# Output sums of a Fourier filter and expert layer with the output weights stationary, turned back by transposing DMAs

## The chip, the cores and the metric

The kernel runs on one core of a Trainium2 chip. The metric is device time in microseconds of one execution, the median of the runs; the profile shows one further execution in detail. A core has a tensor engine (TensorE, "PE" in the profile, with its weight loads as "PEld"), VectorE ("DVE"), ScalarE ("ACT"), GpSimd ("POOL") and SyncE ("SP", which here only issues DMAs). Each takes its instructions from a queue of its own.

## The reference

```python
def _attn_ref(x, filt_r, filt_i):            # x: 8 x 3008 x 256
    X = np.fft.rfft(x, axis=1)
    Y = X * (filt_r + 1j * filt_i)[None, :, :]
    return np.fft.irfft(Y, n=x.shape[1], axis=1)

def _moe_ref(x, w_in, w_out, beta):          # x: 24064 x 256, w_in: 256 x 2048, w_out: 2048 x 256
    h = x @ w_in
    g = h * (1.0 / (1.0 + np.exp(-beta * h)))
    return g @ w_out
```

Each of 8 batches goes through a real Fourier transform along its 3008 tokens, a product with a filter, and the inverse transform. The 24064 tokens then go through a two-layer network with 2048 hidden features and the activation h times sigmoid(beta h).

## The kernel before

The network is the main loop. Tokens are taken in 47 blocks of 512 (`TB`), hidden features in 16 groups of 128 (`NFB`); one block and one group make a step, 752 steps in all. A step `s` computes `hps` (L785: two matmuls, `win_sb` stationary, 512 tokens moving), ScalarE turns it into `gT` (L794, features on partitions, tokens along the row), and two steps later, by `lags`, four matmuls (L803) add the group's share to the output: there the 128 x 128 piece of `gT` is stationary and `wout_sb` (256 columns) moves, so that tokens come out on the partitions of `acc`. After the last group of a block, `out_block` (L753) copies the two banks of `acc` to `ost` on VectorE (L757, shown as L112, the line of the helper) and stores them from SP (L762, L764). `acc` tiles come from a pool of three banks, two of which a block uses. The last block goes through `out_last` instead.

The Fourier work of the next batch is woven into the steps. A table `plan`, filled by `at(step, function, ...)`, is written out by hand (L687 to L735): `s1` (L565) is the first small transform, `a2_load` turns its result by eight transposing DMAs from SP (L581), `s2` (L592) is the second transform and the product with the filter on VectorE (L606, L607, L610), whose two halves are added on GpSimd into `yh` (L611), `s3` (L624) takes `yh` back and stores `z` to DRAM (L631), `zz_load` reads it back turned (L636), and `s4` (L646) makes the tokens of `y` that the main loop reads. Within a step the order of issue is `hps`, then what the plan has, then the output matmuls and, at the end of a block, `out_block`. The engines' queues follow that order. With o the first step of batch b - 1's tokens (0, 80, 176, 272, ... for b = 1, 2, 3, 4), batch b has its `s2` at o + 4, 8 and 12 in each of four blocks, its last `z` store at o + 66, `zz_load` at o + 70, `s4` from o + 80, and `a2_load` for b + 1 at o + 82. Batches 1 and 2 have steps of their own: `a2_load` at 16 and 80, `s2` from 23 and from 88, `zz_load` of batch 1 at 54. Loads of `x` (`load_x`, L171) are issued from GpSimd's queue.

The first batch is done before the steps begin. In that opening the filters, `win_sb` (L476) and the output weights are loaded; `load_wout` (L360) brings four groups of `moe_w_out` into a staging tile `ws` (two of them), `scale_wout` (L367) divides them by beta on GpSimd into `wout_sb`. `spin` (L271) issues filler matmuls on a tile of zeros.

Of the kernel before, what the change touches and what calls it, by code (L numbers as in the profile page):

```python
# [10 lines left out]
P = 128  # L11
# [4 lines left out]
F32 = mybir.dt.float32  # L16
BF16 = mybir.dt.bfloat16
I32 = mybir.dt.int32

TWO_PI = 2.0 * math.pi  # L20

# [15 lines left out]
def kernel(  # L37
# [10 lines left out]
    nc = tc.nc  # L48

    B, S, D = x.shape  # L50
# [20 lines left out]
    tw = dict(reuse_waits="tile")  # L71
# [29 lines left out]
    wout_sb = wpool.tile([P, NFB, D], BF16, name="wout_sb", tag="wout_sb")  # L101
# [4 lines left out]
    st = {}  # L106
# [162 lines left out]
    def spin(n, idle):  # L269
        for _ in range(n):  # L270
            nc.tensor.matmul(idle[:], lhsT=rest[:, :P], rhs=rest[:], start=True, stop=True)  # L271
# [73 lines left out]

    r_sq.close()

    wst = ctx.enter_context(tc.tile_pool(name="wstage", bufs=2, **tw))
    zzpool = ctx.enter_context(tc.tile_pool(name="zzpool", bufs=4, **tw))
    WG = 4  # L350
    wstage = {}

    def load_x(b, g):
        t = xpool.tile([KP, JG, D], BF16, name="xg", tag="xg")
        load_rows(t[:], b, g * JG, (g + 1) * JG)
        xg[b, g] = t

    def load_wout(f0):
        ws = wst.tile([P, WG, D], F32, name="ws", tag="ws")
        nc.sync.dma_start(  # L360
            ws[:],
            moe_w_out[f0 * P : (f0 + WG) * P, :].rearrange("(fb fp) j -> fp fb j", fp=P),
        )
        wstage[f0] = ws
# [117 lines left out]
    load_win(0, 4 * P)  # L482
    spread(4)
    spread(5)
    load_x(1, 0)
    load_win(4 * P, FF)
    for g in range(1, 4):
        load_x(1, g)
    load_wout(0)
    load_wout(WG)  # L490
    scale_wout(0)
    scale_wout(WG)

# [26 lines left out]
    def tail_tile(i, shape, dt=F32):  # L520
        return pair[i].tile(shape, dt, name="pt", tag=f"pt{i}")
# [10 lines left out]
    for e in range(NDC):  # L532
        for h in range(2):
# [1 line left out]
            f4(0, h, e, ps)  # L535
            f4_head(0, h, e, ps, e == 1 and h == 0)
            late.append((0, h, e, ps))
    spin(2, tail_tile(0, [P, 512]))
    z_evac(NUN - 1, 1, s5[1], JG, J, False)
    for a in late:  # L540
        f4_tail(*a, False)
# [145 lines left out]
    for b in range(1, B):  # L687
        o = first_step[b - 1]
        if b == 1:
            at(0, z_late, 1, 0)  # L690
            at(1, z_late, 1, 1)
            s1_steps(1, range(16), [3 + (2 * i + 1) // 3 for i in range(16)], False, (1, 4, 7, 10, 13))
            for i, r in enumerate((2, 3, 4, 5)):
                at(r, f_late, 1, i // 2, i % 2)
            for g in range(NG):
                at(o + 16, a2_load, 1, g)
            for hh, z0, f0 in ((2, (6, 9), (12, 15, 16, 17)), (3, (17, 18), (19, 20, 21, 22))):
                for e in range(NDC):
                    at(z0[e], z_late, hh, e)
                for i, r in enumerate(f0):  # L700
                    at(r, f_late, hh, i // 2, i % 2)
            s23_steps(1, [o + r for r in (23, 25, 27, 29, 31, 34, 36, 38, 40, 42, 44, 46)], 5, 1)
            for h in range(J // JG):
                at(o + 54, zz_load, 1, h)
            s4_steps(1, [o + 66 + (i * 12) // 15 for i in range(16)], 2)
            for f in (2, 3):
                at(f, load_wout, f * WG)
                at(f, scale_wout, f * WG)
            if B > 2:
                for g in range(4):  # L710
                    at(o + 24 + 3 * g, load_x, 2, g)
                late = (54, 55, 56, 57, 58, 59, 60, 61, 66, 67, 68, 70, 72, 73, 74, 76)
                s1_steps(2, range(16), [o + r for r in late], False)
                for g in range(NG):
                    at(o + 80, a2_load, 2, g)
                if B > 3:
                    for g in range(4):
                        at(o + (62, 68, 88, 92)[g], load_x, 3, g)
            continue
        base = [o + 16 * n + s for n in range(4) for s in (4, 8, 12)]  # L720
        if b == 2:
            base[:6] = [o + r for r in (8, 12, 19, 22, 26, 29)]
        s23_steps(b, base, 6, False)
        for h in range(J // JG):
            at(o + 70, zz_load, b, h)
        s4_steps(b, [o + 80 + (i * 13) // 15 for i in range(16)], False)
        if b + 1 < B:
            early = [o + 16 * n + s for n in range(4) for s in (7, 13)]
            late = [o + s for s in (66, 67, 69, 70, 72, 73, 75, 76)]
            s1_steps(b + 1, range(16), early + late, False)  # L730
            for g in range(NG):
                at(o + 82, a2_load, b + 1, g)
            if b + 2 < B:
                for g in range(4):
                    at(o + (30, 62, 88, 92)[g], load_x, b + 2, g)  # L735

    blk = {}
    acc = {}
    lags = {i: (2, 2, 2, 2) for i in range(NBLK)}
    lags[NBLK - 1] = (2, 2, 4, 6)  # L740
    outs = {}
    for s in range(NSTEP):
# [1 line left out]
        for tb, lag in enumerate(lags[i]):  # L744
            outs.setdefault(min(s + lag, NSTEP + max(1, tb)), []).append((i, fb, tb))

    def acc_of(i, tb):
        h = tb if i == NBLK - 1 and tb == 3 else tb // 2
        if (i, h) not in acc:
            acc[i, h] = opsum.tile([P, 2, D], F32, name="acc", tag="acc")  # L750
        return acc[i, h]

    def out_block(i):  # L753
        ost = ostp.tile([P, 4, D], F32, name="ost", tag="ost")
        rows = out[i * TB : (i + 1) * TB, :].rearrange("(c p) d -> p c d", p=P)
        for h in range(2):
            evac(ost[:, 2 * h : 2 * h + 2, :], acc[i, h][:], False)  # L757
        if i < HB:
            for h in range(2):
                off = (i * JG + 4 * h) * D  # L760
                dst = AP(out.tensor, out.offset + off, [[J * D, M], [D, 4], [1, D]])
                nc.sync.dma_start(dst, ost[h * M : (h + 1) * M, :, :])  # L762
            return
        nc.sync.dma_start(rows, ost[:])  # L764

    def out_last(i, tb, ost):
        rows = out[i * TB : (i + 1) * TB, :].rearrange("(c p) d -> p c d", p=P)
        if tb == 1:
            evac(ost[:, :2, :], acc[i, 0][:], True)
            nc.sync.dma_start(rows[:, :2, :], ost[:, :2, :])  # L770
        elif tb > 1:
            evac(ost[:, tb, :], acc_of(i, tb)[:, tb % 2, :], False)
            (nc.scalar if tb == 2 else nc.sync).dma_start(rows[:, tb, :], ost[:, tb, :])

    for s in range(NSTEP + 4):
        if s < NSTEP:
            i, fb = divmod(s, NFB)
            t0 = i * TB
            hps = hpsum.tile([P, TB], F32, name="hps", tag="hps")
            pos = t0  # L780
            while pos < t0 + TB:
                b, n0 = divmod(pos, S)
                ln = min(S - n0, t0 + TB - pos)
                for dc in range(NDC):
                    nc.tensor.matmul(  # L785
                        hps[:, pos - t0 : pos - t0 + ln],
                        lhsT=win_sb[:, dc, fb * P : (fb + 1) * P],
                        rhs=ys[b][:, dc, n0 : n0 + ln],
                        start=(dc == 0),
                        stop=(dc == NDC - 1),  # L790
                    )
                pos += ln
            gT = gpool.tile([P, TB], BF16, name="gT", tag="gT")
            nc.scalar.activation(gT[:], hps[:], ACT.Silu, scale=beta_sb[:, fb : fb + 1])  # L794
            blk[s] = gT
        for fn, a in plan.get(s, ()):
            fn(*a)
        last = NBLK - 1
        if s == NSTEP - 1:
            ost = ostp.tile([P, 4, D], F32, name="ost", tag="ost")  # L800
        for i, fb, tb in outs.get(s, ()):
            lone = i == last and tb > 1
            nc.tensor.matmul(  # L803
                acc_of(i, tb)[:, tb % 2, :],
                lhsT=blk[i * NFB + fb][:, tb * P : (tb + 1) * P],
                rhs=wout_sb[:, fb, :],
                start=(fb == 0 and (tb % 2 == 0 or lone)),
                stop=(fb == NFB - 1),
                skip_group_check=True,
            )  # L810
            if fb == NFB - 1:
                if i == last:
                    out_last(i, tb, ost)
                elif tb == 3:
                    out_block(i)
# [1 line left out]
_INS = ['x', 'filt_r', 'filt_i', 'moe_w_in', 'moe_w_out', 'moe_beta']  # L817
_OUTS = [((24064, 256), 'float32')]
# [25 lines left out]
```

## Time and profile before

| what | value |
|---|---|
| median of 3 runs (range) | 776.09 us (775.89 to 776.11) |
| the profiled execution | 776.16 us |
| its span, first to last instruction | 774.4 us |
| granted TensorE clock over the span | 1.000 |
| TensorE, VectorE, ScalarE, GpSimd busy | 99%, 56%, 71%, 20% |
| bytes moved by DMA | 77.74 MB |

A row of the profile's groups reads: line, engine, operation, what is written and read, shape, count, then busy time in us, mean ns of one, and the idle time of the engine just before, with what ended it. A row of a timeline reads: start in us, us from the first to the end of the last, engine, line, operation, tiles, count; the brackets give idle time before and what ended it. "SPq" is SP's queue issuing a DMA.

### The profile page before, as it was taken

Reading aid. Unit: us, or ns where it says so; the run is one execution under the profiler, and the core shown is the slowest. Engines: PE = TensorE matmul, PEld = TensorE weight load, DVE = VectorE, ACT = ScalarE, POOL = GpSimd, SP = SyncE. Lnnn points to the kernel's source line nnn. Section 1 sums busy time; section 2 is a strip of 40 time slices with the busy share of each in tenths; the row PEclk is TensorE's granted clock in tenths of the full one; section 3 lists DMA queues with packets and bytes.
Section 4 is the critical chain, followed back from the end, with each engine's and each line's share of the span. In section 5 each row is a group of like instructions: output and inputs, shape, how many; then the busy total and the mean of one; then the engine's idle time right before and its main releaser. Section 6 shows DMA issues by size and latency. Waiting matters only on the chain.

```text
span 774.4 us, 15904 instructions
## 1 busy us (share of the span) xinstructions
PE 763.8 (99%) x6384; PEld 550.2 (71%) x6384; DVE 433.0 (56%) x716; ACT 552.2 (71%) x813; POOL 151.0 (20%) x154
## 2 busy tenths in 40 slices
PE   8899999999999999999999999999999999999997
PEld 5677777767777777867778777776777766676665
DVE  8868754766556655566556664566645665321001
ACT  7767877776677776777667777676676777777776
POOL 6714400312012210122201322022200222000000
PEclk9999999999999999999999999999999999999999
DMA  9968575234923248141671317621147111500101
GB/s 200 210 142 133 145 172 110 69 101 93 200 52 74 91 111 180 39 115 50 144 157 55 91 48 176 123 76 48 49 130 137 49 49 48 157 29 28 55 28 55
DMA packets 104125, 77.74 MB, mean 100 GB/s; under 512 B 49692, under 2 KB 97052, under 8 KB 104052
## 3 DMA queue, kind: packets, MB, share of 16 engines
q1 hardware_dynamic: 97652, 63.19, 31.3%
q0 software_dynamic: 4192, 13.40, 10.3%
q8 instruction: 50, 0.82, 0.4%
q10 hardware_dynamic: 2208, 0.14, 0.2%
q14 instruction: 23, 0.19, 0.1%
HBM read 43.46 MB, written 35.65 MB: 102 GB/s over the span
## 4 chain that ended last, share of the span: by engine, by line
PE 94%; DMA 2%; ACT 1%; DVE 1%; POOL 1%; issue 0%; DVEq 0%; POOLq 0%
PE acc L803 42%; PE hps L785 41%; PE ps L646 2%; PE ps L592 2%; PE ps L624 2%; PE ps L565 2%; DMA ws<-in_moe_w_out_dram 2%; POOL wout_sb L367 0%; PE sps L444 0%; ACT aT L110 0%; ACT t L110 0%; ACT y L110 0%; DVE u L226 0%; POOL xg L171 0%; PE sps L423 0%
## 5 line engine op out<-in xcount | busy, mean ns | idle before, releaser
L794 ACT ACTIVATE gT<-hps,beta_sb 128x512 bf16<-128x512 f32 x752 | 516.6, 687 | 209.4 <-PE hps L785 208.2
L803 PE MATMUL acc<-wout_sb,gT 128*128 128x256 bf16 x3008 | 453.2, 272 | 0.7 <-POOL wout_sb L367 0.7
L785 PE MATMUL hps<-y,win_sb 128*128 128x512 bf16 (+7 forms) x1728 | 447.8, 351 | 0.1
L803 PEld LDWEIGHTS <-gT 128*128 128x128 bf16 x3008 | 281.1, 98 | 102.9 <-issue 1.8
L611 POOL TENSOR_TENSOR yh<-a_t,b_t 128x512 bf16<-128x512 f32 x84 | 106.5, 1268 | 419.9 <-DVE b_t L610 419.5
L785 PEld LDWEIGHTS <-win_sb 128*128 128x128 bf16 x1728 | 164.8, 98 | 24.3 <-DVE y L114 0.3
L112 DVE COPY ost<-acc 128x512 f32<-128x512 f32 (+1 forms) x94 | 59.9, 679 | 139.8 <-PE acc L803 139.8
L114 DVE TENSOR_SCALAR y<-ps 128x376 bf16<-128x376 f32 (+2 forms) x128 | 63.3, 510 | 62.8 <-PE ps L646 59.1
L606 DVE TENSOR_TENSOR a_t<-ps,fr_sb 128x512 f32<-128x512 f32 x84 | 58.1, 692 | 67.8 <-PE ps L592 67.2
L112 DVE CAST a<-ps 128x384 bf16<-128x384 f32 x107 | 59.1, 556 | 58.0 <-PE ps L565 47.5
L607 DVE SCALAR_TENSOR_TENSOR b_t<-ps,fi_sb 64x512 f32<-64x512 f32 x84 | 58.2, 693 | 1.1
L610 DVE TENSOR_TENSOR b_t<-ps,fi_sb 64x512 f32<-64x512 f32 x84 | 57.4, 683 | 1.1
L112 DVE CAST z<-ps 128x512 bf16<-128x512 f32 x72 | 49.3, 685 | 1.9 <-PE ps L624 1.0
L646 PEld LDWEIGHTS <-zz 96*128 96x128 bf16 x448 | 29.7, 97 | 22.9
L565 PEld LDWEIGHTS <-xg 94*128 94x128 bf16 x448 | 30.4, 97 | 19.9
L565 PE MATMUL ps<-t,xg 94*128 94x96 bf16 x448 | 36.7, 205 | 0.0
L646 PE MATMUL ps<-t,zz 96*128 96x94 bf16 x448 | 34.7, 205 | 0.0
L592 PE MATMUL ps<-a,t 128*128 128x256 bf16 x168 | 32.1, 273 | 0.0
L624 PE MATMUL ps<-yh,t 128*128 128x256 bf16 x168 | 32.1, 273 | 0.0
L624 PEld LDWEIGHTS <-t 128*128 128x128 bf16 x168 | 16.2, 98 | 17.7 <-issue 0.6
L592 PEld LDWEIGHTS <-t 128*128 128x128 bf16 x168 | 16.1, 98 | 16.1
L171 POOL DMA_DIRECT2D xg<-in_x_dram x24 | 12.5, 524 | 54.9 <-PE ps L565 54.9
(95 smaller groups left out, 177.3 us busy)
## 6 DMA issues: line engine op xcount, KB each, us to landing
out_dram<-ost SPq DMA_DIRECT2D x42, 512.0 KB, 3.0
d<-z SPq DMA_DIRECT2D x28, 384.0 KB, 3.7
zz<-d SPq DMA_DIRECT2D x28, 384.0 KB, 6.8
xg<-in_x_dram POOLq DMA_DIRECT2D x24, 384.0 KB, 4.8
out_dram<-ost SPq DMA_DIRECT2D x9, 256.0 KB, 3.6
ws<-in_moe_w_out_dram SPq DMA_DIRECT2D x4, 512.0 KB, 9.2
fr_sb<-in_filt_r_dram SPq DMA_DIRECT2D x12, 128.0 KB, 4.4
fi_sb<-in_filt_i_dram SPq DMA_DIRECT2D x12, 128.0 KB, 4.3
```

Of the source, the lines that this page charges most:

```text
L112: nc.vector.tensor_copy(dst, src)
L114: nc.vector.tensor_scalar_mul(dst, src, scale)
L565: nc.tensor.matmul(ps[:, m * KP : (m + 1) * KP], lhsT=xg[b, g][:NP, m0 + m, e * P : (e + 1) * P], rhs=t1[:], start=True, stop=True,)
L592: nc.tensor.matmul(ps[:, e, :], lhsT=t2[:, k0 + e, :], rhs=st["a2", b, g][:, kk + e, :], start=True, stop=True,)
L606: nc.vector.tensor_tensor(a_t[:], ps[:], fr_sb[:, ks, :], ALU.mult)
L607: nc.vector.scalar_tensor_tensor(b_t[:M], ps[M:], -1.0, fi_sb[M:, ks, :], ALU.mult, ALU.mult)
L611: nc.gpsimd.tensor_tensor(yh[:], a_t[:], b_t[:], ALU.add)
L624: nc.tensor.matmul(ps[:, e, :], lhsT=t3[:, 2 * i + e, :P], rhs=yh[:, e, :], start=True, stop=True)
L646: nc.tensor.matmul(ps[:, e, :NP], lhsT=zz[:, j0 % JG + e, dc * P : (dc + 1) * P], rhs=t4[:], start=True, stop=True,)
L785: nc.tensor.matmul(hps[:, pos - t0 : pos - t0 + ln], lhsT=win_sb[:, dc, fb * P : (fb + 1) * P], rhs=ys[b][:, dc, n0 : n0 + ln], start=(dc ...
L794: nc.scalar.activation(gT[:], hps[:], ACT.Silu, scale=beta_sb[:, fb : fb + 1])
L803: nc.tensor.matmul(acc_of(i, tb)[:, tb % 2, :], lhsT=blk[i * NFB + fb][:, tb * P : (tb + 1) * P], rhs=wout_sb[:, fb, :], start=(fb == 0 an ...
```

## The change

In all blocks but the last, the output matmul changes its roles: a 128 x 128 piece of `wout_sb` is stationary and the 512 tokens of `gT` move, two matmuls a step instead of four. The sums now stand with output features on partitions and tokens along the row, and have to be turned. `out_turn` copies each bank to `of` in SBUF (VectorE), GpSimd splits the 32-bit numbers into two planes of 16-bit halves (`pl`), and a transposing DMA from SP turns each plane set into `xb`. Six steps later, through the plan, `out_block` has GpSimd join the halves in `ost` and SP store it. The three tiles come from the staging pool `wst`, which gets a third buffer. The opening changes with it: three groups of output weights are loaded at once and the fourth at step 0, the first `x` of batch 1 is loaded after the second part of `win_sb`, one filler matmul goes, and `z_late`, the first four `f_late` and `s1` of batch 1 come a step later.

```diff
-    wst = ctx.enter_context(tc.tile_pool(name="wstage", bufs=2, **tw))
+    wst = ctx.enter_context(tc.tile_pool(name="wstage", bufs=3, **tw))
...
-    load_x(1, 0)
     load_win(4 * P, FF)
-    for g in range(1, 4):
+    for g in range(4):
         load_x(1, g)
-    load_wout(0)
-    load_wout(WG)
+    for f0 in range(0, 3 * WG, WG):
+        load_wout(f0)
     scale_wout(0)
     scale_wout(WG)
...
-    spin(2, tail_tile(0, [P, 512]))
+    spin(1, tail_tile(0, [P, 512]))
...
-            at(0, z_late, 1, 0)
-            at(1, z_late, 1, 1)
-            s1_steps(1, range(16), [3 + (2 * i + 1) // 3 for i in range(16)], False, (1, 4, 7, 10, 13))
-            for i, r in enumerate((2, 3, 4, 5)):
+            at(1, z_late, 1, 0)
+            at(2, z_late, 1, 1)
+            s1_steps(1, range(16), [4 + (2 * i + 1) // 3 for i in range(16)], False, (1, 4, 7, 10, 13))
+            for i, r in enumerate((3, 4, 5, 6)):
...
-            for f in (2, 3):
-                at(f, load_wout, f * WG)
-                at(f, scale_wout, f * WG)
+            at(0, scale_wout, 2 * WG)
+            at(0, load_wout, 3 * WG)
+            at(1, scale_wout, 3 * WG)
...
-    lags = {i: (2, 2, 2, 2) for i in range(NBLK)}
+    lags = {i: (2, 2) for i in range(NBLK)}
     lags[NBLK - 1] = (2, 2, 4, 6)
...
+    def out_turn(i):
+        of = wst.tile([P, NDC, TB], F32, name="ws", tag="ws")
+        pl = wst.tile([P, NDC, 2, TB], U16, name="ws", tag="ws")
+        xb = wst.tile([P, 2, 4, D], U16, name="ws", tag="ws")
+        for dc in range(NDC):
+            evac(of[:, dc, :], acc[i, dc][:].rearrange("p a d -> p (a d)"), False)
+            nc.gpsimd.tensor_copy(
+                pl[:, dc].rearrange("p q t -> p t q"),
+                of[:, dc, :].bitcast(U16).rearrange("p (t q) -> p t q", q=2),
+            )
+            nc.sync.dma_start_transpose(
+                xb[:, :, :, dc * P : (dc + 1) * P].rearrange("p q c d -> p (q c) d"),
+                pl[:, dc].rearrange("p q t -> p (q t)"),
+            )
+        st["xb", i] = xb
+
     def out_block(i):
+        xb = st.pop(("xb", i))
         ost = ostp.tile([P, 4, D], F32, name="ost", tag="ost")
         for h in range(2):
-            evac(ost[:, 2 * h : 2 * h + 2, :], acc[i, h][:], False)
+            cs = slice(2 * h, 2 * h + 2)
+            nc.gpsimd.tensor_copy(
+                ost[:, cs, :].rearrange("p c d -> p (c d)").bitcast(U16).rearrange("p (c q) -> p c q", q=2),
+                xb[:, :, cs, :].rearrange("p q c d -> p (c d) q"),
+            )
...
+            if i < last:
+                nc.tensor.matmul(
+                    acc_of(i, q)[:].rearrange("p a d -> p (a d)"),
+                    lhsT=wout_sb[:, fb, q * P : (q + 1) * P],
+                    rhs=gT[:],
+                    start=(fb == 0),
+                    stop=(fb == NFB - 1),
+                )
+                if fb == NFB - 1 and q == 1:
+                    out_turn(i)
+                    at(s + 6, out_block, i)
+                continue
```

More of the change, by code (lines that the diff above doesn't have):

```diff
@@ L18 @@
 I32 = mybir.dt.int32
+U16 = mybir.dt.uint16
 TWO_PI = 2.0 * math.pi
@@ L745, with acc_of @@
             outs.setdefault(min(s + lag, NSTEP + max(1, tb)), []).append((i, fb, tb))
-    def acc_of(i, tb):
-        h = tb if i == NBLK - 1 and tb == 3 else tb // 2
+    def acc_of(i, h):
         if (i, h) not in acc:
@@ L751, in acc_of, with last_acc @@
         return acc[i, h]
+    def last_acc(tb):
+        return acc_of(NBLK - 1, tb if tb == 3 else tb // 2)
+    def out_turn(i):
[13 more added lines that the diff above has]
+        st["xb", i] = xb
     def out_block(i):
+        xb = st.pop(("xb", i))
         ost = ostp.tile([P, 4, D], F32, name="ost", tag="ost")
-        rows = out[i * TB : (i + 1) * TB, :].rearrange("(c p) d -> p c d", p=P)
         for h in range(2):
-            evac(ost[:, 2 * h : 2 * h + 2, :], acc[i, h][:], False)
+            cs = slice(2 * h, 2 * h + 2)
[3 more added lines that the diff above has]
+            )
         if i < HB:
@@ L763, in out_block @@
             return
-        nc.sync.dma_start(rows, ost[:])
+        nc.sync.dma_start(out[i * TB : (i + 1) * TB, :].rearrange("(c p) d -> p c d", p=P), ost[:])
     def out_last(i, tb, ost):
@@ L771, in out_last @@
         elif tb > 1:
-            evac(ost[:, tb, :], acc_of(i, tb)[:, tb % 2, :], False)
+            evac(ost[:, tb, :], last_acc(tb)[:, tb % 2, :], False)
             (nc.scalar if tb == 2 else nc.sync).dma_start(rows[:, tb, :], ost[:, tb, :])
@@ L800 @@
             ost = ostp.tile([P, 4, D], F32, name="ost", tag="ost")
-        for i, fb, tb in outs.get(s, ()):
-            lone = i == last and tb > 1
+        for i, fb, q in outs.get(s, ()):
+            gT = blk[i * NFB + fb]
+            if i < last:
[10 more added lines that the diff above has]
+                continue
             nc.tensor.matmul(
-                acc_of(i, tb)[:, tb % 2, :],
-                lhsT=blk[i * NFB + fb][:, tb * P : (tb + 1) * P],
+                last_acc(q)[:, q % 2, :],
+                lhsT=gT[:, q * P : (q + 1) * P],
                 rhs=wout_sb[:, fb, :],
-                start=(fb == 0 and (tb % 2 == 0 or lone)),
+                start=(fb == 0 and (q % 2 == 0 or q > 1)),
                 stop=(fb == NFB - 1),
@@ L811 @@
             if fb == NFB - 1:
[L812 to L815, printed above, removed]
+                out_last(i, q, ost)
 _INS = ['x', 'filt_r', 'filt_i', 'moe_w_in', 'moe_w_out', 'moe_beta']
```

## The prediction

> **What bounds the kernel now.** I read the page's busy times first, then the groups of instructions, then TensorE's timeline in a stretch without spectral work.
>
> ```profile
> PE 763.8 (99%) x6384; PEld 550.2 (71%) x6384; DVE 433.0 (56%) x716; ACT 552.2 (71%) x813; POOL 151.0 (20%) x154
> L803 PE MATMUL acc<-wout_sb,gT 128*128 128x256 bf16 x3008 | 453.2, 272 | 0.7 <-POOL wout_sb L367 0.7
> 735.21 0.59 PE L785 MATMUL hps<-y,win_sb 128*128 128x512 bf16 x2
> 735.64 0.60 PE L803 MATMUL acc<-wout_sb,gT 128*128 128x256 bf16 x4
> 736.08 0.59 PE L785 MATMUL hps<-y,win_sb 128*128 128x512 bf16 x2
> L472 POOL COPY fr_sb<-fr_sb 64x1024 f32<-64x1024 f32 x6 | 6.2, 1036 | 2.6 <-DMA fr_sb<-in_filt_r_dram 2.4
> ```
>
> TensorE is busy from end to end and its output matmuls (L803) waited 0.7 us in all. The three timeline rows give the price of one step: the two 512-column matmuls start 0.43 us before the four 256-column ones, and those 0.44 us before the next pair. Start to start, single 512-column matmuls lie 216 ns apart and 256-column ones 109 ns. GpSimd is only 20% busy; L472 is its nearest row for a copy: 1,024 elements a partition in 1.04 us.
>
> Second, the queues that the change loads: the timeline of SP, GpSimd and TensorE at the two places where batch 1 and batch 2 begin their spectral products, and in a later block.
>
> ```profile
> 50.63 11.97 SPq L581 DMA_TRANSPOSE a<-a  x8
> 64.55 1.28 POOL L611 TENSOR_TENSOR yh<-a_t,b_t 128x512 bf16<-128x512 f32 x1 [15.20 <-DVE b_t L610]
> 66.65 1.27 POOL L611 TENSOR_TENSOR yh<-a_t,b_t 128x512 bf16<-128x512 f32 x1 [0.33 <-DVE b_t L610]
> 69.03 0.38 PE L624 MATMUL ps<-yh,t 128*128 128x256 bf16 x2
> ...
> 116.99 12.21 SPq L581 DMA_TRANSPOSE a<-a  x8
> 133.77 1.27 POOL L611 TENSOR_TENSOR yh<-a_t,b_t 128x512 bf16<-128x512 f32 x1 [21.56 <-DVE b_t L610]
> 135.24 0.38 PE L624 MATMUL ps<-yh,t 128*128 128x256 bf16 x2
> ...
> 367.91 1.26 POOL L611 TENSOR_TENSOR yh<-a_t,b_t 128x512 bf16<-128x512 f32 x1 [2.60 <-DVE b_t L610]
> 371.19 0.38 PE L624 MATMUL ps<-yh,t 128*128 128x256 bf16 x2
> 376.35 1.35 SPq L631 DMA_DIRECT2D d<-z  x1
> 380.41 2.06 SPq L636 DMA_DIRECT2D zz<-d  x4
> ```
>
> To see: GpSimd's sum yh ends 1.1, 0.2 and 2.0 us before the L624 matmul that reads it; SP is taken for 12 us by a batch's eight transposes; the z store at 376.35 is what the zz loads wait for. The transposes themselves, by the view of their line and the stage table:
>
> ```profile
> L581 SPq DMA_TRANSPOSE a<-a x56: 1211/1287/2614, 50.6 to 591.8; - x56
> DMA to landing us min/median/max: 2.7/2.8/5.4
> 300.00:309.00 9.00, 9.00 (x92) 6.59 (x89) 5.25 (x10) 6.00 (x9) 0.00 (x0) 1.00 0.90 148
> ```
>
> While they run the DMA engines are 90% busy at 148 GB/s: they are bound by the engines, not by SP's issuing.
>
> **What the Trainium skill says.** "TensorE: Matmul & The Clock Gate", section "Wait — 56ns, not 53.3ns?": a warm matmul costs N / 2.4 GHz plus about 2.5 ns, fixed. The trace agrees (109 = 106.7 + 2.3; 216 = 213.3 + 2.7). "PSUM — Partial Sum Buffer", section "Engine vs sequencer instructions": the queues of ScalarE, VectorE and GpSimdE are strict FIFO; the 419.5 us for which GpSimd stood idle before L611 rows fit that. "GPSIMD Engine Reference", section 7: a read whose step is over 8 bytes costs about 2.9 cycles an element instead of 1.9. No row of before has such a read. "DMA: Bandwidth & Descriptors", section "Latency and other measured facts", has transposing DMAs at 261 GB/s; the trace's 148 decides.
>
> **The change part by part**, against the profiled execution: 776.16 us, of which 774.4 us span.
>
> *Output matmuls.* In 46 of 47 blocks, 16 steps each, four 256-column matmuls become two of 512. Same columns, two fixed costs fewer: 736 steps x 2 x 2.5 ns = 3.7 us (by the medians, 4 x 109 - 2 x 216 = 4 ns a step: 2.9). TensorE sets the end in every step, so this is a gain: **-3.7**. The 98 ns weight loads stay under 216 ns of streaming. PSUM use is as before: two banks a block of three, the first freed at the same point of the boundary.
>
> *Opening.* The 0.7 us wait for wout_sb goes: the third group is loaded with the first two instead of after a buffer came free at 33.1, and the fourth is needed four steps later. The transpose L393 that waited 0.3 us at 34.3 moves behind another hps pair. One 216 ns filler matmul goes, but hps at 33.45 waits for VectorE anyway. Against it, 512 KB of output weights now share the full DMA engines with x of batch 1, which is also queued behind the second part of win_sb: 0 to 1 us. I take **-1.0** (0 to -1.0).
>
> *Copies of the accumulators.* VectorE still makes two 128x512 copies a block (679 ns), now to `of`: **0**.
>
> *GpSimd's work.* Four copies of 1,024 16-bit elements a block: C1 for each of two that split, C2 for each of two that join. Below nothing they can't go; the floor is the 1.04 us of L472, as no row shows 16-bit data going faster. For C1 (contiguous read) the page's 1.9 cycles at its 1.2 GHz give an estimate of 1.6 us as upper end; for C2 (each second read 2,048 bytes away) 2.9 cycles give 2.5. Taking only the page's ratio on the trace's own row, C2 is 1.04 x 2.9 / 1.9 = 1.6. I take **C1 = 1.3, C2 = 1.6**.
>
> *Transposes.* Two a block, 8 tiles of 128x128 against L581's 6: by tiles 1.29 x 8/6 = 1.7 us on SP, 1.77 start to start, landing some 3.3 us after issue.
>
> *An ordinary block.* Take the boundary at 358.90. VectorE's copies end at 359.56 and 360.17. GpSimd splits from 359.65; the first transpose is issued at 359.75 + 1.3 = 361.05, both are issued by 364.6 and landed by 366.1. The joins, in GpSimd's queue between the sums at steps 4 and 8, then run 366.1 to 369.3, and the sum that ran at 367.91 runs 369.3 to 370.6; L624 wants it at 371.19. No stall, 0.6 us left: **0**. The cover is gone when 2 x C2 exceeds 3.8, C2 = 1.9.
>
> *First block of batch 1.* Out transposes of block 0 (step 17) stand in SP's queue behind eight L581 transposes (step 16), which end at 62.6 (s1 one step later, opening earlier: about cancels). So they are issued 62.65 to 66.2 and landed at 67.7. GpSimd's queue reads: first sum, two joins, an x load, second sum. Joins 67.7 to 70.9, load 0.55, second sum to 72.7. L624 wanted it at 69.03, with the opening at 68.0. TensorE waits; net of the opening it is **+3.7** behind (C2 1.04: 2.6; 2.5: 5.5). Behind that sum wait VectorE's next products, through the two a_t, b_t buffers.
>
> *Next boundary, step 33 to 39.* Here seven sums (8.9), four x loads (2.1) and four copies (5.8) fill 16.8 of 17.3 us of GpSimd, and VectorE works back to back from 62.28 to 72.87, so nothing is made up. The joins (3.2) come between two sums with about 1 us of slack, part of the wait hidden: **+1.5** (0.5 to 3.5).
>
> *First block of batch 2.* Same shape: L581's eight end at 129.2, then the two of the block ended at step 81, landed at 134.35; joins to 137.55, x load (which ran at 111.7 before) to 138.1, sum to 139.4, wanted at 135.24: **+4.1** (2.9 to 6.0). For later batches the out transposes stand ahead of L581's and the first products come twelve steps later: 0.
>
> *z store.* Of each batch's last z, queued behind two out transposes. At 374.45 + 0.8 + 1.3 + 3.54 it is issued at 380.1 instead of 376.35, 3.7 us late. First zz use had 2.0 to 4.4 us of slack. In batches 2 to 5 an x load crossed the zz loads (landing 5.6 to 7.6 us against 3.8 without); it now stands behind a later join, which gives about 1.8 back. The last batch has 3.1: **+0.6** (0.4 to 3).
>
> Sum: -3.7 + 3.7 (opening in it) + 1.5 + 4.1 + 0.6 = +6.2. Predicted 776.16 + 6.2 = 782.4 us; the median of 776.09 doesn't move it.
>
> **Rivals.** (1) *GpSimd becomes the pace.* With C1 = 1.6, C2 = 2.5 the joins run 366.4 to 371.4, the sum ends at 372.7, 1.5 us after L624: 23 such blocks (four in each of batches 3 to 7, three in batch 2) give 34 us. With 5.5, 3.5, 6.0 and 3 of the places above, less 3.7: about +48, 824 us. Just over the threshold of 1.9 it is some 795. For it: the join's 2 KB step. Against: L472's 1.04 us lies under the page's 1.6 for a short step already, so the page's prices may be high here. (2) *Faster.* Transposes cost by instruction, not by tile (1.33 us apart, landed 2.8 after issue), and GpSimd's copies by bytes: half of L472's, C = 0.52. Block 0's transposes land at 66.8, its second sum ends at 66.8 + 1.04 + 1.82 = 69.65, 0.6 late; batch 2's at 133.4 + 2.9 = 136.3, 1.0 late; the rest 0.1: -3.7 + 1.7 = -2.0, 774.2. With such transposes it decides below C = 0.57. Against: the engines' 90%, and no GpSimd row that is cheaper for 16 bits. (3) *Nothing in sum.* Such transposes with C = 1.04: -3.7 + 1.7 + 2.0 + 0.4 = +0.4, 776.6. At C = 1.04 with transposes by tile it is 2.6 + 0.5 + 2.9 + 0.4 - 3.7 = +2.7, already in the likeliest case.
>
> **How the numbers follow.** Likeliest, stalls at a few places only, 777.7 to 790: 0.50. GpSimd as the pace, 790 to 830: 0.27. Within 0.2% (1.55 us, about what a measurement of this kernel can tell from no change): 0.08. Faster: 0.15, 771.5 (gain alone) to 774.5. Slower 0.77. Leaving out the top of the second case and the bottom of the faster one gives 773 to 808; the likeliest's own range is 777.7 to 790.
>
> **What would show it.** Output matmuls of 512 columns 216 ns apart; no wait of L803's successor for wout_sb; GpSimd's copies with their means against 1.3 and 1.6; out transposes near 1.7 us on SP; gaps of TensorE before the yh matmuls near 68 to 73 and 135 to 140 us, and few elsewhere. Gaps in every block would be rival 1. The prediction is wrong if the joins take over 1.9 us, if the transposes of block 0 land well before 67 us, or if TensorE stalls at a place not named, the zz matmuls of every batch above all.

## The result: 973.1 us, 25% longer

The changed kernel takes 973.09 us (969.95 to 975.3) against 776.0 for the kernel before on the same chip (four runs now), a ratio of 1.2537 (95% interval 1.25 to 1.2574). The direction was predicted, the size was not: 782.4 us in a range of 773 to 808.

The page of the changed kernel: span, busy times, the granted TensorE clock in 40 slices, and the groups of the output matmul and of GpSimd's two copies (busy us, mean ns of one, idle time before it).

```profile
span 970.2 us, 13236 instructions
PE 807.0 (83%) x4820; PEld 420.0 (43%) x4911; DVE 435.3 (45%) x716; ACT 553.1 (57%) x813; POOL 669.4 (69%) x338
PEclk9997998989999899899989999889998999999998
L761 POOL COPY ws<-ws 128x1024 uint16<-128x1024 uint16 x92 | 426.9, 4851 | 123.8 <-DVE ws L113 123.7
L826 PE MATMUL acc<-gT,wout_sb 128*128 128x512 bf16 x1409 | 448.2, 396 | 4.6 <-issue 1.1
L776 POOL COPY ost<-ws 128x1024 uint16<-128x1024 uint16 x92 | 103.0, 1149 | 144.2 <-DMA ws<-ws 77.5
```

VectorE and ScalarE do what they did. GpSimd went from 151 to 669 us, and 427 of that are the splits (L761): 4.85 us for one, where 1.3 was predicted and 1.6 was the upper end. The join (L776), thought the risky one, takes 1.15. TensorE fell from 99% to 83% busy, and its clock is no longer granted in full. Its waits (what waited for what; us in total, times, longest us):

```profile
PE ps L624 <- POOL yh L611: 105.2, 43, 5.5
PE ps L646 <- DMA zz<-d: 30.3, 7, 5.4
```

and those of SP's queue, the DMA instructions that stood waiting in it:

```profile
SPq L765 <- POOL ws L761: 407.6, 59, 11.5
SPq L786 <- POOL ost L776: 124.0, 31, 6.4
```

So TensorE stands 105 us for GpSimd's sum `yh`, 43 times, and 30 us for the zz tiles, once in each of the seven batches. The second pair says why zz is late: SP stands for a split in front of 59 of the 92 out transposes (the transposing DMAs of the output sums, L765), and for a join in front of 31 stores, and the z store and the zz loads are queued behind them. One boundary between blocks shows how a split becomes a wait, in the timeline of the changed kernel (start in us, us, engine, line; in brackets the idle time before). The rows are grouped by engine:

```profile
452.62 0.68 DVE L610 TENSOR_TENSOR b_t<-ps,fi_sb 64x512 f32<-64x512 f32 x1
...
449.15 9.29 POOL L761 COPY ws<-ws 128x1024 uint16<-128x1024 uint16 x2 [2.87 <-DVE ws L113]
458.02 1.32 POOL L611 TENSOR_TENSOR yh<-a_t,b_t 128x512 bf16<-128x512 f32 x1
...
456.08 0.59 PE L807 MATMUL hps<-y,win_sb 128*128 128x512 bf16 x2
459.39 0.59 PE L624 MATMUL ps<-yh,t 128*128 128x256 bf16 x2 [2.72 <-POOL yh L611]
459.77 1.06 PE L826 MATMUL acc<-gT,wout_sb 128*128 128x512 bf16 x2
```

VectorE had the sum's second operand ready at 452.62 + 0.68 = 453.30. GpSimd was then inside the two splits that began at 449.15, and works in order, so the sum began at 458.02, 4.7 us late. L624, which TensorE reached at 456.67, stood 2.72 us. The last row is a second price: after the gap, two output matmuls take 1.06 us from the start of the first to the end of the second, where a pair before it took 0.59. TensorE runs at half clock: the granted clock is 0.50 from 458.84 for 3.4 us.

A third price stands at the end. The last split, its transposes, its joins and the store run on when TensorE is done:

```profile
954.87 4.95 POOL L761 COPY ws<-ws 128x1024 uint16<-128x1024 uint16 x1
955.82 2.02 PE L837 MATMUL acc<-wout_sb,gT 128*128 128x256 bf16 x17
...
965.27 0.37 SPq L786 DMA_DIRECT2D out_dram<-ost  x1
```

The last matmul ends at 957.8, 12.4 us before the end of the span; in the kernel before it ended at 770.3, 4.1 us before it.

The account of the 195.8 us between the spans (970.2 and 774.4): 105.2 + 30.3 of waits. At half clock the same matmuls take longer: TensorE is busy 807.0 us, where 763.8 less the 3.7 saved, 760.1, were due: 47 us. (The clock says about the same. A mean of 0.941 over 970.2 us means 2 x 0.059 x 970.2 = 114 us at half clock; TensorE had no matmul to run in some 25 of them, and in the other 89 half of the time is lost, 45 us.) The end costs 8.3, and 3.7 go off for the matmuls that went. That is 187; the other 9 are not itemised.

The out transposes, by the view of their line:

```profile
L765 SPq DMA_TRANSPOSE ws<-ws x92: 1232/1233/2503, 61.7 to 959.8; - x92
DMA to landing us min/median/max: 3.0/3.1/5.6
```

1.23 us on SP (1.7 predicted) and 3.1 us to landing (3.3): eight tiles cost SP no more than the six of the batch's transposes did (1.29).

### The profile page after: what moved, and what is told of

The parts are those of the page before. It is cut to its first block, busy times and chain, and to the rows that moved or that the text cites. A ratio compares the mean times of both kernels' runs of the same rounds, so it can differ in the third digit from the quotient of the medians.

```text
span 970.2 us, 13236 instructions
## 1 busy us (share of the span) xinstructions
PE 807.0 (83%) x4820; PEld 420.0 (43%) x4911; DVE 435.3 (45%) x716; ACT 553.1 (57%) x813; POOL 669.4 (69%) x338
## 5 line engine op out<-in xcount | busy, mean ns | idle before, releaser
L761 POOL COPY ws<-ws 128x1024 uint16<-128x1024 uint16 x92 | 426.9, 4851 | 123.8 <-DVE ws L113 123.7
L807 PE MATMUL hps<-y,win_sb 128*128 128x512 bf16 (+7 forms) x1702 | 460.9, 363 | 1.3 <-issue 0.2
L826 PE MATMUL acc<-gT,wout_sb 128*128 128x512 bf16 x1409 | 448.2, 396 | 4.6 <-issue 1.1
L807 PEld LDWEIGHTS <-win_sb 128*128 128x128 bf16 x1728 | 170.3, 101 | 201.5 <-issue 33.3
L776 POOL COPY ost<-ws 128x1024 uint16<-128x1024 uint16 x92 | 103.0, 1149 | 144.2 <-DMA ws<-ws 77.5
L826 PEld LDWEIGHTS <-wout_sb 128*128 128x128 bf16 x1472 | 136.3, 101 | 85.1 <-issue 7.0
L113 DVE COPY ws<-acc 128x512 f32<-128x512 f32 x92 | 59.3, 686 | 145.9 <-PE acc L826 119.6
L624 PE MATMUL ps<-yh,t 128*128 128x256 bf16 x168 | 33.6, 283 | 105.4 <-POOL yh L611 105.2
L624 PEld LDWEIGHTS <-t 128*128 128x128 bf16 x168 | 16.5, 98 | 130.6 <-issue 118.0
L646 PE MATMUL ps<-t,zz 96*128 96x94 bf16 x448 | 37.8, 218 | 30.4 <-DMA zz<-d 30.3
L592 PE MATMUL ps<-a,t 128*128 128x256 bf16 x168 | 34.6, 290 | 0.1
```

Source lines behind the costliest of these rows:

```text
L113: nc.vector.tensor_copy(dst, src)
L646: nc.tensor.matmul(ps[:, e, :NP], lhsT=zz[:, j0 % JG + e, dc * P : (dc + 1) * P], rhs=t4[:], start=True, stop=True,)
L761: nc.gpsimd.tensor_copy(pl[:, dc].rearrange("p q t -> p t q"), of[:, dc, :].bitcast(U16).rearrange("p (t q) -> p t q", q=2),)
L776: nc.gpsimd.tensor_copy(ost[:, cs, :].rearrange("p c d -> p (c d)").bitcast(U16).rearrange("p (c q) -> p c q", q=2), xb[:, :, cs, :].rearr ...
L807: nc.tensor.matmul(hps[:, pos - t0 : pos - t0 + ln], lhsT=win_sb[:, dc, fb * P : (fb + 1) * P], rhs=ys[b][:, dc, n0 : n0 + ln], start=(dc ...
L826: nc.tensor.matmul(acc_of(i, q)[:].rearrange("p a d -> p (a d)"), lhsT=wout_sb[:, fb, q * P : (q + 1) * P], rhs=gT[:], start=(fb == 0), st ...
```

## The experiments

My theory (A): the split is slow because its writes jump. For every 32-bit number it writes one 16-bit half into each plane, 1,024 bytes apart. Written plane by plane, with the jumps in the reads, it would be cheap. The rival (B): a 16-bit copy on GpSimd with any strided operand costs that much, or the cost is the queue that the turn builds on SP and GpSimd, whatever a copy takes.

**The split in another order.** Same bytes to the same places, one plane after the other:

```diff
-                pl[:, dc].rearrange("p q t -> p t q"),
-                of[:, dc, :].bitcast(U16).rearrange("p (t q) -> p t q", q=2),
+                pl[:, dc],
+                of[:, dc, :].bitcast(U16).rearrange("p (t q) -> p q t", q=2),
```

> The changed kernel with one edit: the split of the 32-bit sums into two 16-bit planes walks plane by plane, so that GpSimd writes each plane in one contiguous run and reads every second 16-bit element. Theory A: the 4.85 us of a split come from its writes, which jump 1,024 bytes from element to element; written in runs a split costs what the join costs, about 1.15 us, and the time is the prediction's sum at C1 = C2 = 1.15 with the transposes as the changed kernel showed them (1.28 us apart, landed 3.1 after issue): block 0 of batch 1 2.1 late, batch 2's first 2.5, the dense stretch 0.7, z store 0.4, less 3.7: +2, 778 us (775 to 782), TensorE waiting for yh only near those two places. Theory B: the split is slow because it takes 16-bit elements out of 32-bit ones on GpSimd, in whatever order: still 3 to 5 us each, 890 to 973 us.

Measured: 791.83 us (790.55 to 793.15), ratio 1.0205 (1.0189 to 1.0221). The group of the split on its page, and the wait that remains:

```profile
L761 POOL COPY ws<-ws 128x1024 uint16<-128x1024 uint16 x92 | 93.0, 1041 | 188.2 <-DVE ws L113 188.2
```

```profile
PE ps L624 <- POOL yh L611: 12.8, 5, 5.1
```

4.85 us became 1.04, and 181 of the 197 us went with it: the cause is A's. The time is outside A's range, though: 791.8 is 14 us above the 778 that the prediction's own sum gives with these copies.

**Half of it.** Of the changed kernel's two splits a block, only the second in the new order:

```diff
+                pl[:, dc].rearrange("p q t -> p t q") if dc == 0 else pl[:, dc],
+                of[:, dc, :].bitcast(U16).rearrange("p (t q) -> p t q" if dc == 0 else "p (t q) -> p q t", q=2),
```

> The changed kernel with one of its two splits a block in contiguous runs and the other as it was: 1.04 and 4.85 us. Theory A (GpSimd's queue, in order, sets the loss): of an ordinary block the splits end 6.65 us after the boundary, the transposes land at 9.8, the joins end at 12.1, the next sum at 13.4, its matmul wanted it at 12.3: 1.1 us in each of 23 blocks, 25 us, on top of the 792 of the kernel with both splits in runs; about 815 us (800 to 835), much nearer to that one than to 973. Theory B (the loss follows GpSimd's busy time): halfway, about 880.

Measured: 861.42 us (859.28 to 863.57), ratio 1.1095 (1.1061 to 1.113); waits for `yh` 53.8 us in 26 places, for zz 10.3 in 6, clock 0.974. Half the splits' cost gives less than half of the loss (70 of the 181 us between the two kernels), but this is outside A's range and nearer to B's 880. A had 25 us of new waits where 41 came (53.8 against 12.8), and left out zz and the clock: TensorE is busy 777.2 us instead of 760.1. The account is 53.8 + 10.3 + 17.1 - 3.7 = 77.5 of the 87.4 us between the spans (861.8 and 774.4).

**Is it writes as such, or far writes?** On the first experiment's kernel the join is turned round, so that it writes every second 16-bit element, 4 bytes apart, and reads in runs:

```diff
-                ost[:, cs, :].rearrange("p c d -> p (c d)").bitcast(U16).rearrange("p (c q) -> p c q", q=2),
-                xb[:, :, cs, :].rearrange("p q c d -> p (c d) q"),
+                ost[:, cs, :].rearrange("p c d -> p (c d)").bitcast(U16).rearrange("p (c q) -> p q c", q=2),
+                xb[:, :, cs, :].rearrange("p q c d -> p q (c d)"),
```

> As the kernel with the splits in contiguous runs, and the joins walk plane by plane, so that they read runs and write every second 16-bit element (4 bytes apart). Theory A: only writes that jump far are slow: a join stays near 1.15 us and the time near 792. Theory B: any 16-bit write that isn't contiguous costs as the split did: 4.8 us a join, 950 us or more.

Measured: 797.98 us (797.07 to 798.88), ratio 1.0278 (1.0258 to 1.0299). Its group:

```profile
L776 POOL COPY ost<-ws 128x1024 uint16<-128x1024 uint16 x92 | 118.4, 1332 | 117.0 <-DMA ws<-ws 80.2
```

1.33 us against 1.15: a write step of 4 bytes costs little, and far reads (the join as it was) do as well. Only the far write is dear. Write steps between 4 and 1,024 bytes were not measured.

**The gain alone.** No split, no transposes, no joins; VectorE copies the sums straight to `ost` and SP stores them, with the new matmuls and opening. And the opening alone, on the kernel before.

> The changed kernel without split, transposes and join: VectorE copies the two banks to the store tile at the end of the block and SP stores at once, as before. It leaves out the turning of the output, so rows and columns of the stored sums are not where the reference has them. What stays is the new output matmul and the new opening. Theory: 736 steps x 5 ns = 3.7 us from the matmuls and 1.0 from the opening: 771.4 us (771 to 773), no wait of TensorE for yh. Rival: a 512-column matmul with output weights stationary brings stalls of its own (weight loads, bank use): 774 or more.

> The kernel before with the opening alone changed: three groups of output weights first and the fourth at step 0, the first x load after the second part of the input weights, one filler matmul less, the first z_late, f_late and s1 one step later. Theory: 1.0 us less, 775.1 us (774.8 to 776.1). Rival: the shared DMA engines bring x late and give it back: 776 to 777.

Measured: 771.54 us (771.45 to 773.0), ratio 0.9948 (0.9936 to 0.9961), with no wait for `yh`; and 775.49 us (775.03 to 776.63), ratio 0.9995 (0.9987 to 1.0003), no clear difference. The matmuls' gain of 3.7 us is there (3.95 between the two), and the turn, its split mended, costs 791.8 - 771.5 = 20.3 us.

**Where the 20 us are.** In the mended kernel (the one with the split in its new order) three of the five waits for `yh` lie where the prediction has them, ending at 70.0, 88.9 and 145.3 us; the other two, at 243.7 and 341.0, it does not name. The timeline where batch 2 begins, SP's and GpSimd's rows and then TensorE's:

```profile
123.26 1.11 SPq L784 DMA_DIRECT2D out_dram<-ost  x2
124.47 12.24 SPq L581 DMA_TRANSPOSE a<-a  x8
...
141.30 2.25 POOL L776 COPY ost<-ws 128x1024 uint16<-128x1024 uint16 x2 [11.19 <-DMA ws<-ws]
144.01 1.27 POOL L611 TENSOR_TENSOR yh<-a_t,b_t 128x512 bf16<-128x512 f32 x1
...
145.33 0.58 PE L624 MATMUL ps<-yh,t 128*128 128x256 bf16 x2 [5.06 <-POOL yh L611]
```

The eight transposes of batch 2 began at 116.99 in the kernel before, here at 124.47, 7.5 us later. For 3.9 of these the whole loop is late by now (VectorE copies this block's sums at 127.34 instead of 123.45). For the other 3.6 a store that waits for a join stood ahead of them in SP's queue. The join in turn waited for its out transposes: issued at 111.38 and 112.70, they landed at 118.44 and 120.78, beside a load of `x` under way from 112.28 to 119.81. The transposes of the block that ends here follow, then its joins, then the sum, and TensorE stands 5.06 us. Half clock runs from 142.0 for 6.8 us; nearly half of it falls into the wait itself, and what is left costs 1.7 us more.

That suggests putting the joins later, so that no store waits in SP's queue: `at(s + 12, out_block, i)` instead of `s + 6`.

> As the kernel with the split in contiguous runs, and the joins 12 steps after the end of the block instead of 6, so that in GpSimd's queue they stand behind the sums whose transposes they otherwise wait out. Theory: the waits of the two first blocks and of the dense stretch go, the z store's 0.4 stays: 776.1 - 3.7 - 1.0 + 0.4 = 771.8 us (771 to 774). Rival: the waits were not from the place of the joins but from GpSimd's total work, or a join that waits moves on to another sum: 776 or more.

Measured: 789.12 us (787.03 to 793.28), ratio 1.0184 (1.0156 to 1.0211). A miss: the waits for `yh` fell to 3.3 us, but 3.8 for zz and 6.0 for `a` came up. An out transpose issued at 497.87 landed only at 514.18; four loads of `x`, issued from 497.48 to 499.00, ran beside it.

Next, the stores were moved from SP's queue to GpSimd's: in a first run that alone, in a second with the two joins as steps of their own, eight steps and more behind the end of the block.

> As the kernel with the splits in contiguous runs, and only the stores moved from SP's queue to GpSimd's; joins stay 6 steps behind the block. Theory: of the 20 us over the one without the turn, SP's stores that wait ahead of batch 2's transposes are the part beyond the prediction's places; without them the sum of the prediction holds: 2.1 + 2.5 + 0.7 + 0.4 over 771.5 plus what a slower granted clock after a long gap adds: 777 to 782 us. Rival: the stores are no cause: 790 to 793.

> As the kernel with the splits in contiguous runs, with the stores issued from GpSimd's queue behind its joins, so that SP waits for no join, and with each join on its own place: 8 steps after the end of a block, 10 and 12 for block 0, 8 and 10 for block 1, 12 for the block that ends as batch 2 begins. Theory: what is left of the loss is queues, SP's stores that wait for joins ahead of the next batch's transposes, and joins that wait for transposes ahead of sums. Without both the kernel is at the 771.5 of the one that leaves the turn out, plus 0.5 for the z store: 772 us (771.5 to 774). Rival: the transposes' traffic on the DMA engines is the cause: still 780 or more.

Measured: 817.31 us (809.42 to 817.58), ratio 1.0495 (1.0441 to 1.0549), and 785.63 us (783.21 to 786.65), ratio 1.0115 (1.0096 to 1.0134). Both miss. A store in GpSimd's queue right behind its joins is worse than in SP's: 24.9 us of waits for `yh` and a clock of 0.978. Further back it is a little better.

**Which part of the turn.** Out of the mended kernel, the first leaves the transposes out (the joins read the planes), the second the joins (the store takes `of` at once).

> As the kernel with the splits in contiguous runs, without the transposing DMAs: the joins, still 6 steps after the block, read the split planes directly. It leaves out the turning of the output. GpSimd has the same four copies a block, but no join waits for a DMA. Theory: the 20 us between 791.8 and the 771.5 without any turn come from joins that wait for transposes while sums stand behind them; without these waits 772 us (771.5 to 774). Rival: GpSimd's added busy time is the cause, above all in the dense stretch of batch 1: 780 or more.

> As the kernel with the splits in contiguous runs, without the joins: the transposes run as before, but the store takes the VectorE copy of the sums as it is, at the end of the block. It leaves out the turning of the output. SP's queue and the DMA engines carry the transposes, GpSimd only the splits. Theory as above: 772 to 775 us, TensorE waiting a little for zz and for the second copy of s1, whose buffer the later transposes hold. Rival: the transposes' traffic itself delays z, zz and the next batch's transposes: 780 or more.

Measured: 780.11 us (778.9 to 781.41), ratio 1.0059 (1.0044 to 1.0074), and 785.53 us (782.59 to 786.23), ratio 1.0116 (1.01 to 1.0131). Over the 771.5 without a turn that is 8.6 us for GpSimd's copies and 14.0 for transposes and splits. Both rivals hold: neither part is free. The splits are in both runs, and the second also keeps `of` in its buffer until it is stored, so the share of the transposes alone is not separated.

**Joins where GpSimd is free.** The second of the two kernels that store from GpSimd's queue, with a pool of its own for `xb`, so that a join may be up to 31 steps late, and joins placed where no sum is near.

> As the kernel with joins apart and stores from GpSimd, with two tiles of their own for the transposed planes (and one store tile, one gT and one a2 tile less for the space), so that joins can stand off the sums altogether: block 0 at step 48, block 1 at 51, the two blocks around the start of batch 2 at 104 and 111, a block that ends as a later batch begins 12 steps after, the rest 8. Theory: no join waits ahead of a sum any more; what is left is zz and the buffer of s1: 774 us (772 to 778). Rival: the waits move to other places of SP's and GpSimd's queues: 782 or more.

Measured: 784.74 us (781.9 to 787.91), ratio 1.0112 (1.0091 to 1.0132). Another miss; what is late here is the batch's own transposes, by their line's view:

```profile
L582 SPq DMA_TRANSPOSE a<-a x56: 1214/1307/3520, 52.2 to 605.4; - x56
DMA to landing us min/median/max: 2.7/5.2/9.4
```

The median from issue to landing was 2.8 in the kernel before, and 3.1 in the mended one. Sorted by what was under way between issue and landing, the median in this trace is 2.8 us with neither a load of `x` nor a store (10 transposes), 3.5 with a store (8), 5.9 with a load of `x` (10) and 6.9 with both (21). The kernel before has its loads of `x` in the same steps, but in four batches they ended 0.2 to 0.4 us after the first transpose began, and in the others none ran beside.

**Loads of x away from the transposes.** First the joins near the beginning of a batch were put further off as well, then (second) the loads were placed so that no buffer is filled ahead of its last reader in the order of issue, then (third) the loads alone were moved and the joins put back:

```diff
-                        at(o + (62, 68, 88, 92)[g], load_x, 3, g)
+                        at(o + (58, 106, 122, 138)[g], load_x, 3, g)
...
-                    at(o + (30, 62, 88, 92)[g], load_x, b + 2, g)
+                    at(o + (30, 106, 126 if b == 2 else 122, 138)[g], load_x, b + 2, g)
```

> The kernel with the split in order, the later joins that stand off GpSimd's sums and the stores from GpSimd's queue (784.7 us so far), with one change: the loads of x for a coming batch are issued at steps in which no transposing DMA is under way, and joins near the beginning of a batch stand further off. Theory A: what is left beside the gain of 4.5 us is transposing DMAs that land late because ordinary transfers run beside them. Then the waits of TensorE for VectorE's first transform and for the zz tiles (5 us in the run before, with some 7 us of halved clock after them) go, and the time is 772 to 775 us, below the kernel before. Rival B: the transposes of the sums collide with those of the Fourier work or with the stores themselves, wherever the loads of x stand. Then the time stays at 781 us or above, and the waits only move to other places.

> The kernel before this one (loads of x where no transposing DMA is under way, joins further apart, 775.7 us) with two loads of x moved by a few steps, so that each buffer of x is filled only after the last transform that reads it has been issued. Theory A (late transposing DMAs are what is left): nothing in the collisions changes, 773 to 777 us. Rival B (the late transposes come from collisions that loads of x have no part in, and the run before owed its time to the position of the two loads): 781 us or more.

> The same with the joins back where the run of 784.7 us had them, so that only the loads of x are moved. Theory A: the loads made the transposes late, so most of the 9 us stays gained, 774 to 778 us. Rival B: it was the position of the joins near the beginning of a batch; then 781 to 785 us.

Measured: 775.73 us (773.54 to 779.68), 775.64 (773.55 to 777.32) and 776.74 (774.68 to 780.24), ratios 0.9997 (0.9983 to 1.001), 0.9992 (0.9984 to 1.0) and 1.0007 (0.9995 to 1.0019). The first two leave out the join and store of the last block but one, some 3 us of GpSimd's time near the end; neither is clearly below the kernel before, which the first expectation had. The third leaves out nothing. Its view of the same line, and its longest waits:

```profile
L582 SPq DMA_TRANSPOSE a<-a x56: 1212/1280/2741, 51.8 to 596.0; - x56
DMA to landing us min/median/max: 2.7/2.8/6.4
```

```profile
PE ps L647 <- DMA zz<-d: 1.8, 1, 1.8
...
PE ps L566 <- DMA xg<-in_x_dram: 1.3, 1, 1.3
PE ps L625 <- POOL yh L612: 1.2, 1, 1.2
```

Moving the loads alone (all four of batch 3, three of four of the later batches) took 8.0 us off (784.7 to 776.7), and the landing is back at 2.8 us. The loads of `x` had made the transposes late: A. Most of it is one place. By the start of ScalarE's activation of the same step, the run of 784.7 us lost 8.3 us on the kernel before between steps 90 and 100, where batch 2 begins, and this one 1.4; at the last step they are 9.7 us apart.

**The last 5 us.** The join and stores of the third block 18 steps behind its sums, to clear the way of the zz loads, with the joins of the second run above (all blocks joined and stored); and then the first `x` of batch 1 ahead of the weights again.

> Loads of x apart, joins near the beginning of a batch further off, and the join and stores of the third block 18 steps behind its sums, so that the zz loads of batch 1 no longer run beside those stores; all blocks are joined and stored (the two runs before with the joins further off left out the join and the store of the last block but one). Theory A (transfers that run together are all that is left): the waits of 1.2 us for the sum near 138 us and of 1.8 us for the zz tiles near 107 us go, 773 to 774.5 us, below the kernel before (776.3). Rival B: the stores of the third block are not what made the zz tiles late; then 775.5 to 777 us.

> The same, and the first x of batch 1 is loaded ahead of the second part of the weights of the first layer again, as in the kernel before. The wait of 0.7 to 1.3 us for that x near 38 us should go: 0.7 to 1.3 us below the run beside it, 772 to 773.5 us, if the weights' second part is not needed sooner; if it is, as much is lost at the first matmuls of the steps, and the time is the same.

Measured: 776.99 us (773.35 to 779.66), ratio 1.0008 (0.9998 to 1.0017), and 776.73 us (774.42 to 779.37), ratio 1.0013 (1.0003 to 1.0023). In the first the wait for zz stayed at 1.9 us, so these stores were not what delayed it: the rival. In the profiled execution of the second it went, and so did that for `x`, but 1.5 us of wait for the first layer's weights came, which are now loaded after that `x`. Single executions lie between 773.4 and 779.7 us where the kernel without the turn spans 1.6 us. In the profiled execution of the run of 776.7 us the waits shown above, 4.3 us for zz, `x` and `yh` (0.5 of them, for `x`, are in the kernel without the turn too), are most of the 5.0 us between its span (775.2) and that of the kernel without the turn (770.2); which transfers they come from, and what spreads the executions, stays open. No version beats the kernel before; the best with the turn equal it.

## Why the prediction was wrong

**The step that failed** is *GpSimd's work*: "For C1 (contiguous read) the page's 1.9 cycles at its 1.2 GHz give an estimate of 1.6 us as upper end". The section it drew on ("GPSIMD Engine Reference", section 7) prices steps of reads. The split reads in runs and writes in jumps, so a price for reads was no bound on it. It took 4.84 us (4.72 to 5.00). The text looked for the danger in the join, the copy with the strided read. Everything large follows: at 2 x 4.84 = 9.7 us a block the splits lie across two of GpSimd's sums. This is the mechanism of rival 1, "GpSimd becomes the pace", in 43 places, started by the other copy. So the direction came out right, but not for the reason that the sum gives. Even with the right C1, the prediction's arithmetic counts a stall at its length only; the work lost at half clock (some 45 us) and the longer end (8.3 us) were in no step.

*Output matmuls* (-3.7): right, -3.95. *Opening* (-1.0, 0 to -1.0): -0.4 with an interval of -1.0 to +0.2, inside the range but not told from nothing. *Copies of the accumulators* (0): right, VectorE is busy 435.3 us instead of 433.0.

*C2* (1.6): 1.15, near its floor of 1.04. The trace does not agree with the page's 2.9 cycles for a far read in this copy.

*Transposes* (1.7 us on SP by tiles): 1.23, by instruction, as rivals 2 and 3 assumed. The DMA engines' 90%, read as the bound, did not set SP's time. The landing, 3.1 for 3.3, was right for an undisturbed one; that loads of `x` could double it was in no step.

*An ordinary block* (0): wrong as the change stands, and right for the mended split in all but two blocks. There the 12.8 us of waits for `yh` lie in five places.

*First block of batch 1, the next boundary, first block of batch 2* (+3.7, +1.5, +4.1): in the mended kernel the waits are 1.9 us at 70.0, 2.4 at 88.9, and 0.9 + 5.1 at 139 and 145. The places and the order of SP's queue were right. The store that holds up batch 2's transposes by 3.6 us was missed: the text counted the out transposes in that queue, but not that a store waits there for its join.

*z store* (+0.6): the mended kernel waits 0.5 us for zz; the change as it stands 30.3, behind SP's waits for the splits. "The zz matmuls of every batch above all" was named as what would show it wrong, and did.

Of the mended kernel's 14 us above the 778 of the sum, 12 are accounted for. First block of batch 2: 6.0 us of waits where the sum has 2.5. Next boundary: 2.4 instead of 0.7. Two waits at places not named: 2.1 us at 243.7 and 1.4 at 341.0. Half clock: 10.2 us of it, 3.3 of them in a wait, so 3.4 us. Transposes that land late account for part of these waits; how much was not separated.

## What to carry to other kernels

Price a copy by both its sides. Here far writes were dear and far reads were not, and swapping the loops so that writes run and reads jump was worth a factor of 4.7. When new work goes into an engine's in-order queue, list what waits behind it, stores that wait for a later step included. Count a stall of TensorE of about 2 us or more with the half clock that may follow, and look at what the change adds after the last matmul. Place large loads where no transposing DMA is under way.

## What the runs showed of the hardware

GpSimd, copies of 1,024 16-bit elements a partition: written with jumps of 1,024 bytes 4.84 us; written in runs and read 4 bytes apart 1.04; read with every second element 2,048 bytes away 1.15; written 4 bytes apart 1.33.

The clock: "TensorE: Matmul & The Clock Gate", section "What's actually happening", has it fall to half after an idle window of about 3.4 us. Here half clock came in stretches of 3.4, 6.8 and (in the run with one split mended) 10.2 us, which agrees, but gaps of 2.05 us (at 243.7 in the mended kernel) and 2.72 us (above) were followed by it too. Shorter gaps than the page's can cost a window.

Which gaps do can be read from the traces. The half clock of the changed kernel begins at times a whole number of 3.413 us apart, so cut the run into windows of that length. The gap of 2.72 us above lies with 2.17 us in the window that ends where half clock begins, at 458.84. A gap of the same 2.72 us from 436.55 lies with 1.81 us in one window and 0.91 in the next, and no half clock followed. Cut this way after the first 30 us, and with the ends of matmuls as the profile models them, the traces of all 18 runs have 46 windows at full clock in which TensorE was without a matmul for 2.12 us or more, and half clock followed every one; it followed none with less than 1.8, and 9 of the 19 in between.

Transposing DMAs (of `a`, run of 784.7 us): from issue to landing 2.8 us in the median with neither a load of `x` nor a store under way, 5.9 beside a load of `x`, 6.9 beside a load and a store; in one place of another run 16.3, beside four loads of `x`.
